# One core: windowed attention, downsampled attention and an MLP; 128x128 transposes for four pairs, group sums by selection matrices, a longer ring for the MLP's input, other places for transposes and weights

## Chip, cores and metric

The kernel runs on one core of one Trainium2 chip. The metric is the device time of one execution, in microseconds. TensorE (PE in the profile) multiplies, VectorE (DVE), ScalarE (ACT) and GpSimd (POOL) do elementwise work, and SyncE (SP) issues most DMAs. A DMA can be issued from SP's, ACT's or POOL's instruction queue; all of them share 16 DMA engines.

## What is computed

q, k and v are (8, 8, 576, 64) in float32: batch, heads, positions, width of a head. Two attentions are added and an MLP follows:

```python
q_d = q.reshape(B, H, Sd, factor, D).mean(axis=3)       # factor 4, Sd = 144; k_d, v_d alike
out_up = np.repeat(sm_attn(q_d, k_d, v_d), factor, axis=2)
mask = np.abs(pos[:, None] - pos[None, :]) < factor     # a band of 7
scores = np.where(mask, scale * np.matmul(q, k.transpose(0, 1, 3, 2)), -1000000000.0)
attn_out = out_up + np.matmul(softmax(scores), v)
x = attn_out.transpose(0, 2, 1, 3).reshape(B * S, H * D)   # 4608 x 512
h = x @ w_in                                             # 512 x 2048
out = (h * sigmoid(h)) @ w_out                           # 2048 x 512
```

## The kernel before

**Pairs.** The 64 heads are taken as 32 pairs p of two heads; four pairs make one batch element, that is 576 rows of the MLP's input. For each pair q and k are loaded in float32 (qk), cast to bf16 (qkb), transposed on TensorE (job T, 36 transposes of 64x64, L813) and evicted by ACT and DVE as qT and kT. From these come sums over groups of four positions, qd and kd: for pairs 0 to 11 on TensorE (job G, eight matmuls with an identity, 144 columns each, which read qT and kT), for the others on DVE (L848). Job S computes the scores of the band and of the downsampled part into two PSUM banks; ACT takes the exponentials (Pt and Pd, L896). For pairs 0 to 7 the mask is added in PSUM by four matmuls with 288 columns before the scores; for the others DVE multiplies Pt by a 0/1 mask (L902). Job Z makes the sums of the softmax, whose reciprocals DVE spreads (zt, zr, Rb, L967 to L977). Job PV multiplies by v. DVE scales the product into xo (L993), and POOL adds the two attentions into xT (L1021), the MLP's input, transposed.

**v.** v is loaded twice: in windows of 64 positions (vs, cast to vb on POOL) for the band, and, for pairs 8 and up, in groups of four positions (vq), which POOL sums in two steps (vt, L787, and vd, L792). For pairs 0 to 7 these sums come from vb on TensorE (job VP, nine matmuls).

**MLP.** The 4608 rows are nine tiles of 512. For each tile, 16 units g1 (four 128x512 matmuls each, float32) give the columns of h; ACT takes a tanh (L1047), DVE makes gT of it (L1051). Another 16 units g2 (four 128x512 matmuls in bf16) give the output, which ACT copies out of PSUM (L1079). xT is a ring of XR = 1536 rows, three tiles. A g1 of tile j needs the xT of all pairs of the batch elements that the tile touches: tile 1 needs pairs up to 7, tile 2 up to 11, tile 3 up to 15.

**Order.** Nothing is scheduled at run time. A planner in the kernel (class Plan) holds jobs with costs, due times, pools of buffers and PSUM banks, plays them through, and the instructions of each engine are emitted in the order that it finds; each engine and each queue then runs strictly in that order. DMAs have planned durations (the argument `work`: 0.85 us for q or k of a pair, 0.39 for a quarter of v's windows, 3.2 for a quarter of w_in or w_out), and code has a planned time to be fetched (FETCH), for every 256 instructions of TensorE. Where the plan has TensorE idle early in the run, it puts in matmuls on a constant tile dz, which are thrown away.

Pairs 0 to 7 run as separate jobs. From pair 8 on, one job per pair, the visit V(n), puts S of pair n, T of pair n+1, PV of pair n-2 and Z of pair n-1 together. A visit may run once 8(n - 10) MLP units have been issued.

**Loads.** q and k of a pair are 128 partitions of 576 elements each; k is shifted by half a pair, so that the first pair needs an extra piece, kx. Pairs 1 to 3 are loaded with a cast by the DMA, from POOL's queue (SW). v's windows go to 64 partitions per DMA. The weights go out from POOL's queue; each of the eight parts (w0 to w3 of w_in, w4 to w7 of w_out) waits for a named load of v (W_GATE). The loads of pair 8 wait on SP's queue until w2 has landed.

Of the kernel before, what the change touches and what calls it, by code (L numbers as in the profile page):

```python
# [7 lines left out]
ALU = mybir.AluOpType  # L8
# [10 lines left out]
XR = 1536  # L19
COLD = (8.0, 1.65)  # L20
WARM_END, WARM_GAP, WARM_PART, WARM_COLD = 115.0, 0.4, 0.6, 7.0
FETCH = (4.5, 110.0, 3.7)
N_QK, N_VS, N_VQ, N_QKB, N_VB, N_VD, N_T, N_P, N_ZR, N_RB, N_XO = 3, 4, 2, 5, 5, 5, 3, 4, 2, 4, 2
GS_PE = 12
# [3 lines left out]
CAST2 = 4  # L28
SW = (1, 2, 3)
MB = 8  # L30
LAG = 2
THR0 = 10
# [28 lines left out]
def G1_BANKS(j):  # L61
    return ((6,), (7,), (5,)) if j == 0 else ((6,), (7,), (0,), (1,)) if j == 8 else ((6,), (7,))


def T_BANKS(p):
    return ((4,), (5,), (6,), (7,)) if p < 4 else ((4,), (5,))
# [18 lines left out]
W_GATE = {0: ("lv211",), 1: ("lv511",), 2: ("lv611",), 3: ("lv711",), 4: ("lvq8",), 5: ("lvq9",), 6: ("lvq10",), 7: ("lvq11",)}  # L85
# [6 lines left out]
def load_order():  # L92
    o = ["kx", ("qk", 0), ("qk", 1), ("qk", 2), ("qk", 3), ("v", 0), ("v", 1), ("v", 2), ("v", 3)]
    for p in range(4, NPAIR):
        o += [("qk", p), ("v", p)] + ([("vq", p)] if p >= VP_PE else [])
    return o, {**{p: ["lv311!"] for p in range(4, 8)}, 8: ["w2"]}
# [8 lines left out]
def LD_ENG(x, p):  # L105
    return ("SP", "ACT") if p in (1,) else "SP"
# [388 lines left out]
def bass_hourglass_attn__then__act_silu_kernel(  # L495
# [9 lines left out]
    with kctx:  # L505
# [26 lines left out]
        vq = sb("vq", [128, 4, 256], F32, N_VQ)  # L532
        vt = sb("vt", [128, 4, 128], F32)
        qkb = sb("qkb", [128, 2, 576], BF16, N_QKB)
# [4 lines left out]
        qd = sb("qd", [128, SD], BF16, N_T)  # L539
        kd = sb("kd", [128, 192], BF16, N_T)  # L540
# [6 lines left out]
        for name, n, first in (("qk", N_QK, 0), ("vs", N_VS, 0), ("vq", N_VQ, VP_PE), ("vt", 1, VP_PE),  # L547
                               ("qkb", N_QKB, -1), ("vb", N_VB, 0), ("vd", N_VD, 0), ("T", N_T, 0), ("P", N_P, 0),
                               ("zr", N_ZR, 0), ("Rb", N_RB, 0), ("xo", N_XO, 0), ("th", 2, 0), ("osb", 2, 0)):
            L.pool(name, n, first, SW if name == "qk" else ())  # L550

# [5 lines left out]
        mbias = sb("mbias", [128, 2, 288], BF16)  # L557
        nidn = sb("nidn", [128, 64], BF16)
# [25 lines left out]
        ci, ri = region(1792, 64)  # L584
        kx, rkx = region(2048, 576)
        cpv = cp.rearrange("p (a b) -> p a b", a=2)
        cmv = cm.rearrange("p (a b) -> p a b", a=5)
        CH, CK, CB, CM0, CW, CO, CO2, CE0, CE1, CP_, CM1 = range(11)
# [19 lines left out]
        def fill(name, parts, due, eng=("DVE", "POOL")):  # L608
# [3 lines left out]
            J(name, eng, {"DVE": 0.1 * len(parts), "POOL": (0.14 if name != "rwz" else 0.5) * len(parts)}, emit, due=due)  # L612

        def constants():
            rW = [R(f"hot{i}") for i in range(3)]
            iota("cp", col(CP_), [[1, 1]], 0, 1, rc(CP_), 0.2, -100)
            iota("ci", ci, [[-1, 64]], 0, 1, ri, 0.25, -99)
# [6 lines left out]
            ts("idn", idn[:, :], ci, col(CB), ALU.add, 0.0, ALU.is_equal, rc(CB) + ri, [R("idn")], 0.26,  # L624
               ["ci", "cb"], -98)
# [3 lines left out]
            ts("ce0", col(CE0), col(CP_), 3.0, ALU.is_ge, 1.0, ALU.mult, rc(CP_), rc(CE0), 0.15, ["cp"], 40)  # L629
            ts("ce1", col(CE1), col(CP_), 123.0, ALU.is_lt, 1.0, ALU.mult, rc(CP_), rc(CE1), 0.15, ["cp"], 40)  # L630
# [6 lines left out]
            fill("idwz", [(idw[:, :], 0.0, [], [R("idw")])], -82, "POOL")  # L637
            for j in range(2):
                const(f"idw{j}", "DVE", 0.14, lambda e, j=j: e.tensor_copy(
                    idw[half(j), 64 * j:64 * j + 64], idn[half(j), :]), r=[R("idn"), R("idw")], w=[R("idw")],  # L640
                    pre=["idn", "idwz"] + ["idw0"] * j, due=-81)
            for i, (a, b, c, rr) in enumerate(((0, 58, col(CE0), rc(CE0)), (58, 232, 1.0, []),
                                               (232, 288, col(CE1), rc(CE1)))):
                ts(f"mask{i}", mask[:, a:b], cm[:, a:b], 3.0, ALU.is_le, c, ALU.mult, rr + rm, [R(f"mask{i}")], 0.24,
                   ["cma"] + (["ce0", "ce1"] if rr else []), 41)
            ts("cm0", col(CM0), col(CK), 3.0, ALU.is_lt, 100.0, ALU.mult, rc(CK), rc(CM0), 0.15, ["ck"], -94)
            ts("cm1", col(CM1), col(CK), 59.0, ALU.is_ge, 100.0, ALU.mult, rc(CK), rc(CM1), 0.15, ["ck"], -94)
            ts("nidn", nidn[:, :], idn[:, :], -81920.0, ALU.mult, 0.0, ALU.add, [R("idn")], [R("nidn")], 0.17, ["idn"], -85)
            for i, (y, a, b, c) in enumerate(((0, 0, 58, CM0), (0, 58, 288, None), (1, 0, 232, None), (1, 232, 288, CM1))):
                if c is None:  # L650
                    ts(f"mb{i}", mbias[:, y, a:b], cm[:, a:b], 3.0, ALU.is_gt, 1.0, ALU.mult, rm, [R(f"mb{i}")], 0.42,
                       ["cma"], -84)
                else:
                    ts(f"mb{i}", mbias[:, y, a:b], cm[:, a:b], col(c), ALU.add, 3.0, ALU.is_gt, rc(c) + rm, [R(f"mb{i}")],
                       0.3, ["cma", "cm0", "cm1"], -84)
# [10 lines left out]
            for i in range(N_VQ):  # L666
                fill(f"vqz{i}", [(vq[i][:, t, :], 0.0, [], [R(f"vqc{i}{t}")]) for t in (1, 3)], 100)
# [5 lines left out]
        def rows(t, p, n, off):  # L673
            return bass.AP(tensor=t.tensor, offset=t.offset + (128 * p + off) * 576, ap=[[576, n], [1, 576]])
# [7 lines left out]
        def loads(p, order):  # L682
            if p == 0:
# [118 lines left out]
        def t_home(p, x, r):  # L802
            return bank(("qk"[x], p))[0], 32 * r
# [481 lines left out]
```

## Time and profile before

| | us |
|---|---|
| three runs | 367.11, 366.29, 366.30 |
| median | 366.3 |
| profiled execution | 365.78 |
| its span in the profile | 364.0 |

Busy time by stage, from the stretches of the trace. The first stage ends with the first transposes, the second with the scores of pair 4, the third with the first visit (pair 8), the fifth holds two visits, and the sixth ends with the last transposes.

| stretch, us | PE busy | DVE busy | ACT busy | POOL busy | clock | GB/s |
|---|---|---|---|---|---|---|
| 0 to 8.96 | 5.52 | 5.67 | 3.71 | 6.32 | 1.00 | 176 |
| 8.96 to 30.28 | 17.53 | 14.40 | 9.86 | 9.97 | 0.84 | 238 |
| 30.28 to 61.09 | 29.20 | 21.26 | 18.89 | 18.53 | 1.00 | 251 |
| 61.09 to 141.08 | 77.02 | 65.73 | 48.50 | 63.18 | 1.00 | 236 |
| 141.08 to 162.04 | 13.16 | 6.63 | 6.12 | 13.51 | 0.76 | 235 |
| 162.04 to 240.29 | 77.54 | 59.15 | 44.99 | 40.62 | 1.00 | 118 |
| 240.29 to 364.00 | 119.69 | 47.35 | 47.17 | 4.82 | 1.00 | 43 |

The clock is the share of full speed that TensorE was granted. GB/s is what all DMAs moved. In the timeline views a row has the start, the duration, the engine, the line, the operation with what it writes and reads, and in brackets how long the engine stood idle before it and which event ended that. Rows of SPq are the issuing of DMAs on SP's queue. Rows follow program order within an engine, and neighbours of one form are merged.

### The profile page before, as it was taken

The numbers are of one execution on the slowest core, as the hardware profiler recorded it, in microseconds if no ns is written. First come the engines' busy times: TensorE is split into PE (matmuls) and PEld (weight loads), VectorE is DVE, ScalarE is ACT, GpSimd is POOL, SyncE is SP. The second block draws the span as 40 slices with busy tenths as digits, with TensorE's granted clock in tenths as the row PEclk, the third lists the DMA queues.
The fourth block names the chain that finished last, engine by engine and source line by source line (L and its number), as shares of the span: only waits on it lengthen the run. The fifth ranks groups of instructions, "written<-read, shape, count | busy, mean of one in ns | idle before, by whom it ended". The sixth has DMA issues, their size and how long they took to land.

```text
span 364.0 us, 10850 instructions
## 1 busy us (share of the span) xinstructions
PE 339.7 (93%) x4674; PEld 217.9 (60%) x4709; DVE 220.2 (60%) x398; ACT 179.2 (49%) x328; POOL 156.9 (43%) x183
## 2 busy tenths in 40 slices
PE   6969899999989999199999999999999999999996
PEld 2747677676556666066666666666665666655542
DVE  6667577668887795257868786776544233433300
ACT  4625566666465566045565546554344343444311
POOL 6349258768986863956658535100310000000000
PEclk9898999999999999779999999999999999999999
DMA  8999999999978786988873100000001001100112
GB/s 177 175 296 252 211 289 247 250 262 272 264 207 231 216 237 175 273 226 234 223 239 96 68 31 33 31 31 29 31 31 58 30 31 41 46 29 31 57 60 86
DMA packets 70522, 52.78 MB, mean 145 GB/s; under 512 B 45898, under 2 KB 56394, under 8 KB 70474
## 3 DMA queue, kind: packets, MB, share of 16 engines
q1 hardware_dynamic: 64378, 44.66, 44.6%
q0 software_dynamic: 5088, 7.18, 9.1%
q8 instruction: 37, 0.61, 0.7%
q10 hardware_dynamic: 1008, 0.25, 0.3%
q14 instruction: 11, 0.09, 0.1%
HBM read 45.61 MB, written 9.44 MB: 151 GB/s over the span
## 4 chain that ended last, share of the span: by engine, by line
PE 87%; DVE 4%; DMA 3%; issue 3%; ACT 2%; POOL 0%; SPq 0%; DVEq 0%; ACTq 0%; POOLq 0%
PE PS L571 84%; DMA qk<-in_k_dram 3%; PE PS L813 3%; DVE xo L993 1%; DVE gT L1051 1%; ACT th L1047 1%; DVE Rb L977 1%; POOL xT L1021 0%; ACT Pt L896 0%; ACT qT L565 0%; ACT osb L1079 0%; SPq L678 0%; DVE zt L967 0%; ACT qkb L565 0%; DVE zr L971 0%
## 5 line engine op out<-in xcount | busy, mean ns | idle before, releaser
L571 PE MATMUL PS<-xT,w_in_sb 128*128 128x512 f32 x576 | 164.5, 422 | 8.7 <-DVE gT L1051 8.5
L1051 DVE SCALAR_TENSOR_TENSOR gT<-th,PS 128x512 bf16<-128x512 f32 x144 | 97.2, 681 | 86.0 <-ACT th L1047 81.3
L1047 ACT ACTIVATE th<-PS 128x512 f32<-128x512 f32 x144 | 86.3, 600 | 109.5 <-PE PS L571 109.3
L571 PE MATMUL PS<-w_out_bf,gT 128*128 128x512 bf16 x547 | 131.1, 381 | 3.3 <-ACT qT L565 1.0
L571 PEld LDWEIGHTS PS<-xT,w_in_sb 128*128 128x128 f32 x576 | 106.8, 191 | 38.1 <-DVE gT L1051 11.0
L571 PEld LDWEIGHTS PS<-w_out_bf,gT 128*128 128x128 bf16 x576 | 51.2, 98 | 70.3 <-issue 14.0
L1021 POOL TENSOR_TENSOR xT<-xo 128x576 fp32r<-128x576 f32 (+3 forms) x48 | 42.8, 908 | 60.7 <-DVE xo L993 31.0
L1079 ACT ACTIVATE osb<-PS 128x512 f32<-128x512 f32 x36 | 21.5, 597 | 46.7 <-PE PS L571 46.7
L774 POOL CAST qkb<-qk 128x1152 bf16<-128x1152 f32 x28 | 33.0, 1178 | 11.8 <-DMA qk<-in_k_dram 11.8
L993 DVE TENSOR_TENSOR xo<-PS,Rb 128x720 f32<-128x720 f32 x32 | 28.7, 896 | 14.9 <-POOL xT L1021 9.1
L565 POOL CAST vb<-vs 128x640 bf16<-128x640 f32 x32 | 23.2, 727 | 28.8 <-PE PS L571 17.4
L787 POOL TENSOR_TENSOR vt<-vq 128x512 f32<-128x512 f32 x24 | 31.5, 1313 | 4.8 <-DMA vq<-in_v_dram 4.6
L977 DVE STREAM_TRANSPOSE Rb<-zr 128x768 f32<-128x768 f32 x32 | 30.9, 966 | 0.2
L896 ACT ACTIVATE Pt<-PS 128x576 bf16<-128x576 f32 x32 | 20.7, 647 | 5.5 <-PE PS L571 5.5
L565 ACT ACTIVATE qT<-PS 128x576 bf16<-128x576 bf16 x30 | 19.9, 667 | 5.2 <-PE PS L813 5.2
L813 PE MATMUL PS<-idn,qkb 64*64 64x64 bf16 x1152 | 16.3, 196 | 3.6 <-ACT qkb L565 2.0
L792 POOL TENSOR_TENSOR vd<-vt 128x256 bf16<-128x256 f32 x24 | 18.2, 759 | 0.0
L902 DVE TENSOR_TENSOR Pt<-Pt,mask 128x576 bf16<-128x576 bf16 x24 | 16.6, 691 | 2.6 <-ACT Pt L896 2.6
L565 ACT ACTIVATE kT<-PS 128x576 bf16<-128x576 bf16 x27 | 17.9, 663 | 0.0
L896 ACT ACTIVATE Pd<-PS 128x432 bf16<-128x432 f32 x32 | 17.2, 536 | 0.0
L813 PEld LDWEIGHTS PS<-idn,qkb 64*64 64x64 bf16 x1152 | 13.1, 110 | 4.9 <-ACT qkb L565 2.1
L571 PE MATMUL PS<-Pd,vd 64*64 64x72 bf16 (+1 forms) x256 | 14.3, 201 | 0.5 <-issue 0.5
(64 smaller groups left out, 230.9 us busy)
## 6 DMA issues: line engine op xcount, KB each, us to landing
vs<-in_v_dram SPq DMA_DIRECT2D x123, 80.0 KB, 4.5
out_dram<-osb SPq DMA_DIRECT2D x36, 256.0 KB
qk<-in_q_dram SPq DMA_DIRECT2D x29, 288.0 KB, 4.2
qk<-in_k_dram SPq DMA_DIRECT2D x28, 288.0 KB, 5.0
vq<-in_v_dram SPq DMA_DIRECT2D x24, 256.0 KB
w_in_sb<-in_moe_w_in_dram POOLq DMA_DIRECT2D x4, 1024.0 KB, 8.6
w_out_bf<-in_moe_w_out_dram POOLq DMA_DIRECT2D x4, 512.0 KB, 9.7
vq<-in_v_dram SPq DMA_DIRECT2D x48, 32.0 KB
```

The costliest lines, as they stand in the source:

```text
L565: return e.activation(out_, in_, AF.Copy) if eng == "ACT" else e.tensor_copy(out_, in_)
L571: P.op("PE", lambda t: t.matmul(out_, lhsT, rhs, start=start, stop=stop, skip_group_check=True), r, w)
L774: P.op("POOL", lambda e, a=i(), b=j(): e.tensor_copy(qkb[b][:, :, :], qk[a][:, :, :]), [R(f"qk{i()}0"), R(f"qk{i()}1")], [R(f"qkb{j()}0"), ...
L787: P.op("POOL", lambda g: g.tensor_tensor(vt[:, :, :], vq[n][:, :, 0:128], vq[n][:, :, 128:256], ALU.add), [R(f"vqm{n}"), R(f"vqe{n}0"), R( ...
L813: P.op("PE", lambda e, o=o, w=w, j=j: e.transpose(o, w, idn[half(j), :]), [R("idn"), R(f"qkb{n}{x}")], [rB[t]])
L896: P.op("ACT", lambda e: e.activation(d[:, :, :], PS[:, b[0]:b[1] + 1, a:e_], AF.Exp, scale=sc), [rB[b[0]], rB[b[1]]], [R(f"P{m}" if local ...
L977: P.op("DVE", lambda e: e.transpose(Rb[n][:, :].rearrange("p (c q) -> p c q", q=32), zr[z][:, :].unsqueeze(2).to_broadcast([128, 24, 32])) ...
L993: P.op("DVE", lambda e: e.tensor_tensor(xo[x][:, :, :], PS[:, bb[0]:bb[1] + 1, 0:360], Rb[u][:, :].rearrange("p (x c) -> p x c", x=2)[:, : ...
L1021: P.op("POOL", lambda g, dst=dst, in0=in0, in1=in1: g.tensor_tensor(dst, in0, in1, ALU.add), [R(f"xo{x}")], xblk(kc, t + a, t + e_))
L1047: P.op("ACT", lambda e: e.activation(th[x][:, :], PS[:, b, :], AF.Tanh, scale=0.5), [rB[b]], [R(f"th{x}")])
L1051: P.op("DVE", lambda e: e.scalar_tensor_tensor(gT[j % 2][:, f, :], th[x][:, :], 1.0, PS[:, b, :], ALU.add, ALU.mult), [rB[b], R(f"th{x}")] ...
L1079: P.op("ACT", lambda e, s=S("osb", n), b=bank(key)[0]: e.activation(osb[s][:, :], PS[:, b, :], AF.Copy, scale=0.5), [rB[bank(key)[0]]], [R ...
```

## The change

- Layout of loads: q of a pair goes to partitions 0 to 63 and k to partitions 64 to 127, the two heads side by side in the free dimension (128 runs of 2304 bytes, as before). The shift of k, the extra piece kx and the casting loads of pairs 1 to 3 are gone; those pairs are cast on POOL. qkb is laid out as [128, 9, 2, 64], so that for each of nine positions both heads are 128 contiguous columns.
- T of pairs 0 to 3 is nine transposes of 128x128, into two banks (E, F or G, H); the others keep 36 of 64x64.
- G reads qkb instead of qT and kT: nine matmuls with 288 columns, by nine selection matrices `sel`, made on DVE at the start (in the memory that vq uses later). It is used for pairs 0 to 7 (GS_PE 12 to 8); pairs 8 to 11 take DVE's sums. One copy of 288 columns takes the place of two of 144.
- The mask bias is two matmuls of 128 rows and 288 columns instead of four of 64 rows.
- From pair 4 on, T is a job of its own, in the score banks 0 and 1, and may run once 8(p - 10) - 12 MLP units have been issued. g1 may use banks 4 to 7 instead of 6 and 7.
- XR is 2048: four tiles.
- W_GATE: w1 to w4 each wait for an earlier load of v than before, and w5 to w7 follow w4 at once. Pair 8's loads wait for w3.
- vt is gone: POOL's first sum over vq is written in place. Pools: four vd for five, four T for three, two Rb for four.
- The planner's DMA durations of loads and weights are multiplied by DSLOW = 1.2, its code fetch times are longer (FETCH), and two rules of its choice among TensorE's jobs are gone.

```diff
-XR = 1536
+XR = 2048
-FETCH = (4.5, 110.0, 3.7)
-N_QK, N_VS, N_VQ, N_QKB, N_VB, N_VD, N_T, N_P, N_ZR, N_RB, N_XO = 3, 4, 2, 5, 5, 5, 3, 4, 2, 4, 2
-GS_PE = 12
+FETCH = (5.2, 110.0, 4.5)
+DSLOW = 1.2
+N_QK, N_VS, N_VQ, N_QKB, N_VB, N_VD, N_T, N_P, N_ZR, N_RB, N_XO = 3, 4, 2, 5, 5, 4, 4, 4, 2, 2, 2
+GS_PE = 8
+TW = 3
-CAST2 = 4
-SW = (1, 2, 3)
+CAST2 = 1
+TAHEAD = 12
 def G1_BANKS(j):
-    return ((6,), (7,), (5,)) if j == 0 else ((6,), (7,), (0,), (1,)) if j == 8 else ((6,), (7,))
+    return ((6,), (7,), (0,), (1,)) if j == 8 else ((6,), (7,), (5,), (4,))
 def T_BANKS(p):
-    return ((4,), (5,), (6,), (7,)) if p < 4 else ((4,), (5,))
+    return ((0,), (1,)) if p > TW else (EF, GH) if p < 4 else (EF,)
-W_GATE = {0: ("lv211",), 1: ("lv511",), 2: ("lv611",), 3: ("lv711",), 4: ("lvq8",), 5: ("lvq9",), 6: ("lvq10",), 7: ("lvq11",)}
+W_GATE = {0: ("lv211",), 1: ("lv411",), 2: ("lv511",), 3: ("lv611",), 4: ("lv711",), 5: ("w3!",), 6: ("w4!",), 7: ("w5!",)}
-    return o, {**{p: ["lv311!"] for p in range(4, 8)}, 8: ["w2"]}
+    return o, {**{p: ["lv311!"] for p in range(4, 8)}, 8: ["w3"]}
 def LD_ENG(x, p):
-    return ("SP", "ACT") if p in (1,) else "SP"
+    return ("SP", "ACT") if (x, p) == ("v", 1) else "ACT" if (x, p) == ("k", 0) else "SP"
...
+            for i in range(9):
+                ts(f"sel{i}", sel[:, i, :], ci, ch_[:, i:i + 1], ALU.is_equal, 1.0, ALU.mult, ri + rh, [R(f"sel{i}")], 0.45,
+                   ["ci", "cgf"], -80)
...
-        def rows(t, p, n, off):
-            return bass.AP(tensor=t.tensor, offset=t.offset + (128 * p + off) * 576, ap=[[576, n], [1, 576]])
+        def rows(t, p):
+            return bass.AP(tensor=t.tensor, offset=t.offset + 128 * p * 576, ap=[[576, 64], [64 * 576, 2], [1, 576]])
...
         def pe_T(p):
+            n = S("qkb", p)
+            if wide(p):
+                b = bank(("t", p))
+                for r in range(9):
+                    o = PS[:, b[r // 8], 64 * (r % 8):64 * (r % 8) + 64].bitcast(BF16)
+                    P.op("PE", lambda e, o=o, r=r: e.transpose(o, heads(n, r), idw[:, :]),
+                         [R("idw"), R(f"qkb{n}0"), R(f"qkb{n}1")], [rB[b[r // 8]]])
+                return
...
         def pe_G(p):
-            s, b = S("T", p), bank(("g", p))[0]
-            for x, t in enumerate((qT[s][:, :], kT[s][:, 3:579])):
-                for r in range(4):
-                    mm(PS[:, b, 144 * x:144 * x + 144], idw[:, :], t.rearrange("p (g r) -> p r g", r=4)[:, r, :],
-                       [R("idw"), R(f"{'qk'[x]}T{s}")], [rB[b]], r == 0, r == 3)
+            n, b = S("qkb", p), bank(("g", p))[0]
+            for r in range(9):
+                mm(PS[:, b, 0:288], heads(n, r), sel[:, r, :], [R(f"sel{r}"), R(f"qkb{n}0"), R(f"qkb{n}1")], [rB[b]], r == 0, r == 8)
...
                 for h in range(2):
-                    for y in range(2):
-                        mm(PS[half(y), bb[h], 0:288], nidn[half(h), :], mbias[half(h), y, :],
-                           [R("nidn")] + [R(f"mb{i}") for i in range(4)], [rB[bb[h]]], True, False)
+                    mm(PS[:, bb[h], 0:288], idw[:, :], mbias[:, :], [R("idw"), R("mbias")], [rB[bb[h]]], True, False)
...
+        def one_T(p):
+            J(f"T{p}", "PE", 0.7 if wide(p) else 0.42 if p <= SPLIT else 0.55, lambda jb: pe_T(p), mm=9 if wide(p) else 36, kind="A" if p <= SPLIT else "T", due=D(p, 8.5),
+              thr=8 * (p - THR0) - TAHEAD, take=[("T", p)] if p > SPLIT else [], **tk(p))
+            after_T(p)
```

In the program that this gives, the first visit's scores stand after 17 MLP units (16 before), those of pairs 9, 13, 17 and 20 after 35, 59, 87 and 104 units (20, 40, 61 and 76 before); the filler matmuls are 20 for 29, the last four of them just before the first visit.

## The prediction

> **What bounds the kernel now.** I read the slices first, to see where TensorE is not at work, then the two timelines around the holes, then stretches by stage.
>
> ```profile
> PE 339.7 (93%) x4674; PEld 217.9 (60%) x4709; DVE 220.2 (60%) x398; ACT 179.2 (49%) x328; POOL 156.9 (43%) x183
> ...
> PE   6969899999989999199999999999999999999996
> ...
> PEclk9898999999999999779999999999999999999999
> DMA  8999999999978786988873100000001001100112
> GB/s 177 175 296 252 211 289 247 250 262 272 264 207 231 216 237 175 273 226 234 223 239 96 68 31 33 31 31 29 31 31 58 30 31 41 46 29 31 57 60 86
> ```
>
> TensorE is the bound almost everywhere; slice 17 (146 to 155 us) is empty, and its clock is low there and after. The early slices are thinner too, and the DMA engines are full up to about 100 us.
>
> ```profile
> 140.28 0.43 SPq L678 DMA_DIRECT2D qk<-in_k_dram  x1
> ...
> 145.15 1.14 POOL L774 CAST qkb<-qk 128x1152 bf16<-128x1152 f32 x1 [5.50 <-DMA qk<-in_k_dram]
> 145.41 0.43 SPq L678 DMA_DIRECT2D qk<-in_k_dram  x1
> ...
> 149.60 1.14 POOL L774 CAST qkb<-qk 128x1152 bf16<-128x1152 f32 x1 [0.75 <-DMA qk<-in_k_dram]
> 150.71 2.37 POOL L1021 TENSOR_TENSOR xT<-xo 128x576 fp32r<-128x576 f32 x2
> ...
> 152.01 0.91 DVE L993 TENSOR_TENSOR xo<-PS,Rb 128x720 f32<-128x720 f32 x1 [9.10 <-POOL xT L1021]
> ...
> 154.96 3.78 PE L571 MATMUL PS<-xT,w_in_sb 128*128 128x512 f32 x8 [7.73 <-DVE gT L1051]
> ```
>
> This is the big hole, read backwards. TensorE waits 7.73 us for gT; DVE, in order, has stood 9.10 us before an xo product, for want of an xo buffer; POOL, in order too, stood before two casts whose q and k had not landed, with the xT sums that free xo queued behind them. So a late load of a pair needed later stops work that was ready. Then eight matmuls take 3.78 us (2.11 at 142.5): the clock row is 0.50 to 159.5 us, which is another 2.4 us. Together 10.1 us.
>
> ```profile
> 8.22 0.68 ACT L565 ACTIVATE qkb<-qk 128x576 bf16<-128x576 f32 x1 [2.81 <-DMA qk<-in_k_dram]
> ...
> 19.76 0.41 PE L571 MATMUL PS<-Pd,vd 64*64 64x72 bf16 x6 [0.47 <-issue]
> ...
> 25.90 0.18 PE L571 MATMUL PS<-Pt,vb 64*64 64x56 bf16 x1 [2.62 <-issue]
> ...
> 43.44 0.31 PE L813 MATMUL PS<-idn,qkb 64*64 64x64 bf16 x14 [1.29 <-issue]
> ```
>
> Counting a weight load and a matmul as one instruction each in program order, the "issue" waits (with 0.31 at 35.83) stand at instructions of about 702, 958, 1470 and 1726: a grid of 256. The queue of instruction loads has 37 loads, 0.61 MB, for TensorE's 9,383 instructions. So these are waits for code, 4.7 us, with a half clock (0.50) from 26.3 to 30.3 behind the longest, about 2 us more. The time from one such point to the next is 4.9 to 7.6 us where it decides.
>
> **Prices on TensorE at full clock** (start of one block to the next in the timeline): an MLP unit of four 128x512 matmuls 0.91 us (49 matmuls in 11.15); 36 small transposes T 0.31; group sums G 0.94 (46.47 to 47.41); scores with mask bias 0.50; sums Z 0.37; VP 0.62; PV 0.40; a late visit 1.44. Check: up to the first visit at 61.09 the work is 8 pairs x 3.14 = 25.1, T and G of pair 8 1.25, 16 units 14.6, start 8.96: 49.9, so 11.2 us are waits and slow clock. From there to the end (361.5) 272 units are 247.5 and the visits 35.0, three G 2.8, thirteen filler matmuls 2.9: 288.2 of 300.4, so 12.2 us are lost, 10.1 of them in the big hole.
>
> **The change, part by part.**
>
> *Wide transposes, pairs 0 to 3.* 9 instead of 36, so 54 instructions fewer each, 216 in all. The trace has no 128x128 transpose; nearest is VP, nine matmuls with 128 columns at 0.62. By the 36 small ones as floor 0.31, by G's 0.117 each as ceiling 1.05; I take 0.62, so +1.2 us on TensorE for four.
>
> *Group sums by selection matrices.* Nine matmuls over 288 columns in place of eight over 144, for 8 pairs, not 12. A 512-column one takes 0.2275, so 288 take 0.128, and nine 1.1 us (floor 0.94 as now, ceiling 1.4): +1.3 over 8 pairs, and G of pairs 8 to 11 is gone: -3.8. G now reads qkb, not the evicted qT and kT, so it no longer waits for 1.3 us of evictions before each early score block. Pairs 8 to 11 pay two DVE sums of 0.71 each, less a 0.31 copy: 4.4 us on DVE, which is 82% busy from 61 to 141 (65.73 of 79.99) with TensorE then idle only 3 us; I count nothing, 2 us if the cover is gone. Bias: two 288-column matmuls for four concurrent quarter ones, 0.25 for 0.15, +0.8.
>
> *Loads.* The kx load (0.74) and the six casting loads on POOL's queue (2.09 to 5.46) go; q0 and k0 go out first, on SP and ACT. Now k0 goes out third and lands 6.22 later. First issues here landed after 3.1 (half the size) to 6.2; I take 4.5, so casts at 5.3 and T0 at 6.6, for DVE makes six of nine selection matrices before its cast (0.33 to 0.66 each by the vsel and mbias rows). The first G, at half clock, is twice its price, so of 2.4 us gained at T0 I keep 1.0 at the first scores (-2.5 to +1). Casts of pairs 1 to 3 on POOL, 3 x 1.15, fall into its idle 6.95 to 14.03; the memsets of vq, 1.54, move behind the last G into POOL's idle 38.3 to 45.2, with casts behind them.
>
> *w_out ahead of pair 8.* POOL issues w_in's last part and the four of w_out in a row (0.78 each, in the same idle time). SP's queue, with everything of pair 8 and on behind it, waits for w_in3 and not w_in2. It stood 9.8 us until 43.44, and then the DMA engines were empty (share 0.08 at 42 to 44). Pairs 0 to 7 and w_in are 11.7 MB; at 255 to 277 GB/s (the rate of 18 to 42 us) they are in by 46 to 49 us. Pair 8 took 17.7 us from issue to its visit, with 8 us of that unforced; so the visit is at 57 to 62.
>
> *First stage, summed.* Start 6.6, four pairs at 3.7 and four at 3.4, T 0.3, 17 units 15.5: 50.8. Of 11.2 us lost I leave 8: fewer code points (the fourth pair ends near instruction 800, not 1100) but fillers and the wait for pair 8. First visit at 58.8 with 17 units done, 57.9 by the old 16: **-3.2**.
>
> *Later stages.* G of pairs 9 to 11 **-2.8**; thirteen fillers fall to four, which stand before the visit and were counted: half of 2.9 is **-1.4**, since part of it was waiting anyway. The planner's DMA times are now 20% longer: before, a late pair of 1.25 MB was planned at 4.1 us (305 GB/s), while the stretches from 60 to 100 us moved 248 to 270; now 253. So casts stand in POOL's order nearer to when they can run, and the ring of 2048 lets xT sums go on further ahead: the hole **-10.1**.
>
> *New waits.* Transposes now use the score banks: scores, two exponentials 1.19, T 0.31, two evictions 1.34, a DVE sum 0.7 and four handovers make some 4.6 us between visits, and the tightest new visits (4 units apart) leave 4.9; a tanh of 0.6 in between costs its length. Attention also runs 15 to 20 units later: MLP tile 2 needs pair 11, and all 64 earlier units are used up just as it comes. Pair 13's scores (at 105 us) stand before that, and want by some 95 us pairs 0 to 7 7.3 MB, w_in 4.2, w_out 2.1, five and a half later pairs 6.9, seven outputs 1.8, code 0.4: 22.7 MB, where the old order had moved 24.5 by 100 (the GB/s row): slack of about 2 us at worst, 6 at best. Pair 9's vq load must wait on SP's queue for pair 8's to land, once, some 4.5 us, ahead of all later loads. Rb has two buffers for four. I take **+4** (0 to 10).
>
> Sum: 364.0 - 3.2 - 2.8 - 1.4 - 10.1 + 4 = 350.5 span. The profiled execution took 365.8, 1.8 more than its span, and the median of the runs shown is 0.5 above that: **352.8**, say 352.5.
>
> [...]
>
> **Rivals.**
>
> *A hole of the old kind comes back* (a load late by some us with sums queued behind it, around w_out's loads or tile 2). For it: the DMA share is 0.9 to 1.2 to 100 us, and slack is 2 to 6 us. Against: loads are ordered by a rate that the trace shows. It costs 5 to 10 more: 357 to 363.
>
> *Half-partition loads are slower.* q goes to partitions 0 to 63 only and k to 64 to 127, where each took 128. If such a load ran at half rate, the 8.3 MB of q and k that pair 13 needs would take 31 us longer at 265 GB/s, of which slack covers 6: 25 on top of 352.5, 377. It decides once it costs more than 14, that is 22.7 MB at under some 210 GB/s. Against: v's loads go to 64 partitions already, and the DMA engines move 250 and more with them.
> [...]
>
> *All of it works*: new waits 0, first stage -6: 345 to 346.
>
> *The early part gains nothing* because loads, not code, pace it: 355 to 356, still in the forecast's band.
>
> **Chances.** Forecast band 348 to 357 0.52; better 0.14; a hole again 0.19; half-partition loads or a starved tile 2 that costs more than the 14 gained 0.15, of which 0.03 ends within 0.3% (1.1 us, about what a measurement can tell). So faster 0.85, same 0.03, slower 0.12. Range 345 to 363.
>
> **What would show it.** Right: no idle of over 3 us on TensorE after 100 us, POOL's casts waiting less than 2 us on loads; G at about 1.1 us and wide T at 0.6; first visit near 59; "issue" waits under 3 us. Wrong: q and k landing later than the 4.2 to 5.0 us of now, TensorE idle around 60 to 110 us before pair 8 or MLP tile 2.

## The result, and the profile after

| | us |
|---|---|
| changed kernel, four runs | 375.29, 377.4, 378.57, 379.5; median 377.99 |
| kernel before, four runs | median 366.34 |
| ratio | 1.0305, 95% interval 1.0242 to 1.0367 |
| profiled execution, its span | 375.29, 373.1 |

Slower by 3.1%, where 352.5 was forecast. The page after (TensorE's row, the slices of 9.3 us, one queue's share, and the median us from issue to landing of q and k):

```profile
PE 343.0 (92%) x4508; PEld 214.6 (58%) x4552; DVE 228.1 (61%) x400; ACT 177.7 (48%) x313; POOL 156.9 (42%) x192
...
PE   6687899999998698979996999999999999999996
...
PEclk9999899999999899989998999999999999999999
DMA  8999989948987999988899452120000100010112
GB/s 180 198 245 236 267 184 219 220 118 213 233 220 205 236 213 222 198 231 217 189 236 273 120 134 89 46 68 28 32 28 30 56 28 30 37 47 30 38 74 84
...
q1 hardware_dynamic: 64746, 46.06, 51.2%
...
qk<-in_q_dram SPq DMA_DIRECT2D x32, 288.0 KB, 4.9
...
qk<-in_k_dram SPq DMA_DIRECT2D x31, 288.0 KB, 5.5
```

The one empty slice is gone, and in its place TensorE is thinned out in many (slices 13, 14, 16, 18 and 22, within 112 to 205 us). The loads carry less: from 60 to 80 and 80 to 100 us all DMAs moved 196 and 191 GB/s, before 248 and 270. Queue q1 carries what SP issues, the loads of q, k and v and the stores. Before, the page had

```profile
q1 hardware_dynamic: 64378, 44.66, 44.6%
```

Now the queue took 51.2% of 16 engines for 46.06 MB; times the span that is 0.512 x 373.1 / 46.06 = 4.15 us of 16 engines for a MB, before 0.446 x 364.0 / 44.66 = 3.64. So each MB costs 14% more of the engines' time. That is not all: the engines were also less busy, at a share of 1.03 and 0.80 in these two stretches where it was 1.19 and 1.07 before.

The first pairs in the timeline (start, duration, engine, line, operation, and the idle time before with its end):

```profile
6.83 0.67 PE L807 MATMUL PS<-idw,qkb 128*128 128x128 bf16 x9 [0.63 <-DVE qkb L568]
7.34 1.27 PE L574 MATMUL PS<-vqa,qkb 128*128 128x288 bf16 x9
10.14 0.68 PE L807 MATMUL PS<-idw,qkb 128*128 128x128 bf16 x9 [1.53 <-POOL qkb L763]
10.66 1.27 PE L574 MATMUL PS<-vqa,qkb 128*128 128x288 bf16 x9
11.76 0.41 PE L574 MATMUL PS<-mbias,idw 128*128 128x288 bf16 x2
```

From block to block the wide T takes 0.51 (6.83 to 7.34), G 1.10, the bias 0.34. But T1 waits 1.53 us for its cast on POOL, T2 1.00 and T3 1.06. The first visit comes at 68.94 with 17 units done (61.09 with 16 before). Now SP's queue, with the ACT and POOL rows that belong to it:

```profile
72.86 0.60 SPq L681 DMA_DIRECT2D qk<-in_q_dram  x1
73.50 0.61 SPq L681 DMA_DIRECT2D qk<-in_k_dram  x1
74.15 1.93 SPq L707 DMA_DIRECT2D vs<-in_v_dram  x3
...
81.35 0.60 ACT L1080 ACTIVATE osb<-PS 128x512 f32<-128x512 f32 x1 [2.87 <-PE PS L574]
81.97 0.38 SPq L681 DMA_DIRECT2D out_dram<-osb  x1
82.39 0.60 SPq L707 DMA_DIRECT2D vs<-in_v_dram  x1
...
84.67 0.60 SPq L681 DMA_DIRECT2D qk<-in_q_dram  x1
85.05 0.72 POOL L568 CAST vb<-vs 128x640 bf16<-128x640 f32 x1 [5.52 <-DMA vs<-in_v_dram]
```

The first output store stands on SP's queue from 76.08, and what it stores is ready at 81.95. Behind it stands the last quarter of a v load that is already out by three quarters; POOL waits 5.52 us for it, with the casts of later pairs behind. Pair 11's q goes out at 84.67, 11.8 us after pair 10's. (Pair 10's had itself gone out 12.8 us after pair 9's, with no store between: four loads of v took SP 6.24 us there, and it waited 2.5 us before a vq load.) The loss reaches TensorE at 124 us:

```profile
119.53 0.72 POOL L568 CAST vb<-vs 128x640 bf16<-128x640 f32 x1 [1.47 <-DMA vs<-in_v_dram]
...
122.09 1.26 POOL L778 TENSOR_TENSOR vqa<-vqa 128x512 f32<-128x512 f32 x1 [1.83 <-DMA vqa<-in_v_dram]
123.31 1.20 POOL L1022 TENSOR_TENSOR xT<-xo 128x576 fp32r<-128x576 f32 x1
...
124.56 0.50 PE L574 MATMUL PS<-xT,w_in_sb 128*128 128x512 f32 x1 [3.28 <-POOL xT L1022]
```

This is the form of the old hole, smaller: an xT sum stands on POOL behind work that waits for v (1.47 and 1.83 us), TensorE has used up all its units and waits 3.28 us, and the clock sags behind it (0.91 from 120 to 140). TensorE waits again at 145.46 (1.74 us, for a cast of POOL), 165.35 (1.85) and 199.56 (3.29).

### The profile page after: what moved, and what is told of

Read it like the earlier page. It is cut to its first block, busy times and chain, and to the rows that moved or that the text cites. A ratio compares the mean times of both kernels' runs of the same rounds, so it can differ in the third digit from the quotient of the medians.

```text
span 373.1 us, 10580 instructions
## 1 busy us (share of the span) xinstructions
PE 343.0 (92%) x4508; PEld 214.6 (58%) x4552; DVE 228.1 (61%) x400; ACT 177.7 (48%) x313; POOL 156.9 (42%) x192
## 3 DMA queue, kind: packets, MB, share of 16 engines
q1 hardware_dynamic: 64746, 46.06, 51.2%
## 4 chain that ended last, share of the span: by engine, by line
PE 54%; DMA 17%; SPq 12%; POOL 8%; issue 5%; DVE 1%; ACT 0%; POOLq 0%; DVEq 0%; ACTq 0%
PE PS L574 53%; DMA vqa<-in_v_dram 7%; DMA qk<-in_k_dram 6%; SPq L707 5%; DMA vs<-in_v_dram 4%; SPq L681 3%; SPq L721 3%; POOL vqa L778 2%; POOL xT L1022 2%; SPq L717 2%; POOL qkb L763 2%; POOL vd L783 1%; PE PS L815 1%; POOL vb L568 1%; ACT osb L1080 0%
## 5 line engine op out<-in xcount | busy, mean ns | idle before, releaser
L574 PE MATMUL PS<-xT,w_in_sb 128*128 128x512 f32 x576 | 170.1, 428 | 9.6 <-POOL xT L1022 9.6
L574 PEld LDWEIGHTS PS<-xT,w_in_sb 128*128 128x128 f32 x576 | 107.4, 192 | 39.3 <-POOL xT L1022 11.8
L574 PEld LDWEIGHTS PS<-w_out_bf,gT 128*128 128x128 bf16 x576 | 49.2, 98 | 66.2 <-issue 17.3
L1022 POOL TENSOR_TENSOR xT<-xo 128x576 fp32r<-128x576 f32 (+5 forms) x48 | 43.0, 909 | 32.2 <-DVE xo L994 32.1
L763 POOL CAST qkb<-qk 128x1152 bf16<-128x1152 f32 x31 | 35.7, 1150 | 34.8 <-DMA qk<-in_k_dram 34.8
L778 POOL TENSOR_TENSOR vqa<-vqa 128x512 f32<-128x512 f32 x24 | 30.8, 1282 | 23.2 <-DMA vqa<-in_v_dram 23.2
L994 DVE TENSOR_TENSOR xo<-PS,Rb 128x720 f32<-128x720 f32 x32 | 28.6, 895 | 11.9 <-PE PS L574 11.8
L568 POOL CAST vb<-vs 128x640 bf16<-128x640 f32 x32 | 22.9, 722 | 12.4 <-DMA vs<-in_v_dram 12.3
L852 DVE TENSOR_REDUCE qkd<-qT 128x144 bf16<-128x576 bf16 x24 | 17.5, 727 | 9.0 <-ACT qT L568 9.0
L783 POOL TENSOR_TENSOR vd<-vqa 128x256 bf16<-128x256 f32 x24 | 17.9, 746 | 9.9 <-PE PS L574 9.2
L815 PEld LDWEIGHTS PS<-idn,qkb 64*64 64x64 bf16 x1008 | 10.7, 111 | 14.5 <-issue 4.7
L852 DVE TENSOR_REDUCE qkd<-kT 128x144 bf16<-128x576 bf16 x24 | 17.5, 731 | 0.0
L815 PE MATMUL PS<-idn,qkb 64*64 64x64 bf16 x1008 | 13.9, 198 | 3.5 <-POOL qkb L763 1.7
```

The costliest lines, as they stand in the source:

```text
L568: return e.activation(out_, in_, AF.Copy) if eng == "ACT" else e.tensor_copy(out_, in_)
L574: P.op("PE", lambda t: t.matmul(out_, lhsT, rhs, start=start, stop=stop, skip_group_check=True), r, w)
L763: P.op("POOL", lambda e, a=i(), b=j(): e.tensor_copy(qkb[b][:, :, :, :].rearrange("p r h d -> p h r d"), qk[a][:, :, :].rearrange("p h (r ...
L778: P.op("POOL", lambda g: g.tensor_tensor(a, a, b, ALU.add), vr(n), [R(f"vqs{n}")])
L815: P.op("PE", lambda e, o=o, w=w, x=x: e.transpose(o, w, idn[half(x), :]), [R("idn0"), R("idn1"), R(f"qkb{n}0"), R(f"qkb{n}1")], [rB[t]])
L852: P.op("DVE", lambda e: e.tensor_reduce(dst, src.rearrange("p (g r) -> p g r", r=4), AX.X, ALU.add), [R(f"{'qk'[x]}T{s}")], [R(f"{'qk'[x]} ...
```

## The experiments

Ratios are to the kernel before, measured beside each run on the same chip, with their 95% interval; its median was 366 to 369 us there. "Full rows", the halves in the kernel before and the first even/odd run mix rows: scores are then taken between wrong rows of q and k, with every instruction otherwise as it was.

**Full rows in the changed kernel, halves in the kernel before.** Two runs, each with the order of all engines unchanged. (In the kernel before, the casts of single tiles then also wait for both loads of a pair.)

```diff
-  [[576, 64], [64 * 576, 2], [1, 576]]  into  qk[...][half(x), :, :]
+  [[576, 128], [1, 576]]                into  qk[...][:, x, :]
```

> The changed kernel, same order on every engine, but q and k of a pair again go to all 128 partitions each, one row of 2304 bytes per partition, instead of q to 0..63 and k to 64..127. It puts rows of q and k in other places than the transposes want, so the scores are those of mixed rows; the work and its order are unchanged. Layout theory (a load to half of the partitions is slower: in the changed kernel SP issues one in 0.61 us instead of 0.43 and the DMA share per MB of SP's queue is 11% higher): issue back to 0.43, first visit at 62 to 65 us instead of 68.9, time 364 to 370. Order theory (the gate on w3, the vq buffers and the output stores in SP's queue make the loads late): first visit within 1 us of 68.9, time 376 to 379.

> The kernel before, same order, with q and k of pairs 0 and 4 to 31 loaded to half of the partitions each, two rows of 2304 bytes per partition (the rows then stand in other places than the transposes want; the work is unchanged). Layout theory: slower than before by 5 to 12 us, the hole near 146 us longer, landing times of q and k up by 0.5 us or more. Order theory: 366 to 368.

Full rows: 363.51 us, 0.9873 [0.978, 0.9966]. Halves put into the kernel before: 379.27, 1.0294 [1.0215, 1.0374]. The two go opposite ways by 4.3 and 2.9%. With full rows the page has

```profile
q1 hardware_dynamic: 64746, 46.06, 45.9%
...
qk<-in_q_dram SPq DMA_DIRECT2D x32, 288.0 KB, 4.3
...
qk<-in_k_dram SPq DMA_DIRECT2D x31, 288.0 KB, 5.1
```

which is 0.459 x 361.9 / 46.06 = 3.61 us for a MB, against 4.15; the halves in the kernel before took 0.495 x 377.0 / 44.81 = 4.17:

```profile
q1 hardware_dynamic: 64442, 44.81, 49.5%
```

So the layout is a cause. It leaves 361.7 (0.9873 x 366.3) where 352.5 was forecast. The rate is no sign of the layout alone: with full rows 60 to 80 us moved only 128 GB/s, while SP stood 12.4 us before a store.

**The planner's slower transfers alone**, in the kernel before.

```diff
-  0.85 * n / 128   (and the other durations of loads)
+  0.85 * DSLOW * n / 128,  DSLOW = 1.2
```

> The kernel before with one thing of the change: the planner's DMA durations times 1.2, so only the order of instructions on the engines and the fillers differ. If the hole at 146 us comes from an order made with too fast loads, as the prediction held: no idle of over 3 us on TensorE after 100 us and 354 to 360 us. If the order is not what makes the hole, or the fillers and the later visits that the longer durations bring cost as much: 364 to 370.

360.91 us, 0.98 [0.972, 0.9879], and again below; after 100 us no wait of TensorE is over 1.7 us. So planning with slower transfers cures the big hole.

**The weight gates.** Before's W_GATE, and pair 8 behind w2: once in the changed kernel, once with full rows as well.

```diff
-W_GATE = {..., 1: ("lv411",), ..., 5: ("w3!",), 6: ("w4!",), 7: ("w5!",)};  8: ["w3"]
+W_GATE = {..., 1: ("lv511",), ..., 5: ("lvq9",), 6: ("lvq10",), 7: ("lvq11",)};  8: ["w2"]
```

> The changed kernel with the gates of before: w1 to w3 one load of v later, w_out gated by pairs 8 to 11's vq loads, pair 8 waiting for w2. The order follows the new plan. Order theory: pair 8's loads go out near 44 us instead of 54.4, first visit near 62, time 368 to 373. Layout theory: loads stay late, and w_out now lands late as well, so TensorE waits after 32 units: 376 to 385.

> The changed kernel with the q and k loads over all 128 partitions (rows mixed as in the run with full rows), and besides with the weight gates of the kernel before: w_in pieces after the v loads of pairs 2, 5, 6, 7, w_out after the sums' loads of pairs 8 to 11, pair 8 waiting for the third piece of w_in. Everything else of the change is kept and the order is planned anew. Theory A (what is left of the miss after the layout, 363.5 against a forecast of 352.5, is mostly the first stage, held up by weights that were moved ahead of pair 8): pair 8's loads go out at 43 to 45 us instead of 47.7, the first visit is near 61 instead of 66, and the time is 356 to 359 us. Theory B (the first stage is held by the POOL casts and the code waits, and weights only take other bytes' place): first visit at 64 to 67 us, time 361 to 366 us.

In the changed kernel 371.93, 1.0111 [1.0015, 1.0208], first visit 63.66 for 68.94. With full rows 361.32, 0.9839 [0.9753, 0.9925], against 0.9873 without: no difference that the intervals allow to be told, though the first visit moved from 65.96 to 62.34. So the gates cost 2% with halves and nothing that shows with full rows.

**Even and odd partitions.** Same order, same rows to as many partitions, only other ones:

```diff
-  qk[S("qk", p)][half(x), :, :]
+  qk[S("qk", p)][x:128:2, :, :]
```

> The changed kernel, instruction for instruction in the same order; only the partitions differ to which the q and k loads write: q of a pair goes to the 64 even partitions and k to the 64 odd ones, instead of q to the lower half and k to the upper half. Number of loads, rows per load, bytes per row and partitions per load (64) stay. The rows of q and k are then interleaved in the tiles that are transposed and grouped, so scores are taken between mixed rows. [...]

371.7 us, 1.0167 [1.0079, 1.0256]: neither the time of full rows (363.51) nor that of halves (377.99). The page says what came back and what did not:

```profile
q1 hardware_dynamic: 64746, 46.06, 44.8%
...
qk<-in_q_dram SPq DMA_DIRECT2D x32, 288.0 KB, 4.2
...
qk<-in_k_dram SPq DMA_DIRECT2D x31, 288.0 KB, 4.8
```

The transfer is at 0.448 x 368.0 / 46.06 = 3.58 us for a MB, as with full rows, and landing too. The issue on SP is 0.62, as with halves (0.43 with full rows). What differs between halves and this is which 64 partitions; so the transfer's price lies in their lying side by side. But only 1.4% of time came back (1.0305 to 1.0167, whose intervals just overlap) of the 4.3% that full rows gain with the same order and the same transfer. The rest goes with two rows for each of 64 partitions. The longer issue fits it: from pair 11's q to pair 16's SP takes 34.45 us here and 32.38 with full rows, and ten issues that are 0.19 longer make 1.9. That it is the reason is not shown.

A MB costs more in adjacent halves (4.15 us) and not on every second partition (3.58; full rows 3.61); why, no run shows. All of q1 loses 15% a MB; q and k, 63 loads of 288 KB, are 18.6 of its 46.06 MB, and if they bear all of it, a MB of theirs costs some 37% more (an estimate from 4.15, 3.61 and these sizes).

**Stores from ACT's queue.** In this run and the one with full rows SP stood over 12 us before the first store, so the next runs move the 36 stores to ACT, which makes what they store. The order of TensorE, DVE and POOL is kept in both.

```diff
-  P.op(j.ran, lambda s: s.dma_start(out_(), in_()), ...)
+  P.op("ACT" if name[:3] == "out" else j.ran, lambda s: s.dma_start(out_(), in_()), ...)
```

> The changed kernel with one difference: its 36 output stores are issued from ACT's queue, behind the copy that feeds them, instead of from SP's. The order of TensorE, DVE, POOL and of all that is left on SP is the same; ACT's has the stores added (0.33 us each on SP). Nothing of the computation differs. Theory A (in the changed order a store stands on SP's queue before its data are ready, with loads behind it: SP stood 5.9 us before the first store at 76 us, and later pairs' casts and xT sums waited for those loads): loads of pair 11 and on go out some 6 us earlier, TensorE's waits on POOL's xT fall from 9.6 to under 4 us, and the time is 366 to 372 us. Theory B (the transfers themselves, at 191 to 196 GB/s from 60 to 100 us, are the limit, and an earlier issue only queues them earlier): 375 to 380 us.

> The changed kernel with the q and k loads over all 128 partitions (rows mixed as in the run with full rows, 363.5 us) and the 36 output stores issued from ACT's queue instead of SP's; all else in the same order. There SP stood 12.4 us before the first store, and the stretch from 60 to 80 us moved 128 GB/s. Theory A (that stop is what makes the 3.8 us wait for a cast at 134 us and the low clock behind it): GB/s of 60 to 80 us back over 220, no wait on POOL's qkb or xT over 1.5 us after 100 us, 354 to 359 us. Theory B (the rest of the miss is the first stage alone, first visit at 66 instead of 58.8, and the loads are early enough): 361 to 366 us.

The changed kernel with this alone: 365.43 us, 0.9933 [0.9891, 0.9975], against 1.0305. With full rows as well: 356.19, 0.9682 [0.9613, 0.9752]. SP's queue in the first of the two (its profiled execution took 369.3, the longest of its ten):

```profile
69.66 0.61 SPq L681 DMA_DIRECT2D qk<-in_q_dram  x1
70.31 0.61 SPq L681 DMA_DIRECT2D qk<-in_k_dram  x1
...
76.10 0.60 SPq L681 DMA_DIRECT2D qk<-in_q_dram  x1
76.75 0.60 SPq L681 DMA_DIRECT2D qk<-in_k_dram  x1
...
82.01 0.60 SPq L681 DMA_DIRECT2D qk<-in_q_dram  x1
```

In these rows a pair goes out every 6 us, with no gap of 11.8, and all DMAs move 229 and 230 GB/s from 60 to 80 and 80 to 100 us although the layout is still that of halves. So the low rates of the changed kernel there came of the store too. TensorE's waits at 124, 145 and 165 us are gone, and the one near 200 is left (5.1 us at 193.6). The first visit is later than in the changed kernel (72.27 for 68.94) in this faster run, so what the stores cost lies behind it. With full rows 60 to 80 us move 252 GB/s, and no wait of TensorE after 100 us is over 0.9. Theory A of both runs holds (365.43 lies just under its range); its sign of small xT waits does not in the first run's profile (6.5 us).

**The same in the kernel before**, with the planner's slower transfers, and these alone once more.

> The kernel before, planned with the DMA durations times 1.2, and its 36 output stores issued from ACT's queue instead of SP's; all else in the same order. It computes all that the reference does. Theory A (stores and waits on SP hold loads there too: 3.9 us before stores, 6.1 before vq loads from 60 to 200 us): 1 to 4 us faster than the same kernel with the stores on SP, in the same call. Theory B (loads run far enough ahead, and ACT, which makes the exponentials and tanh, loses 12 us of issuing): 0 to 3 us slower.

> The kernel before, planned with the DMA durations times 1.2 alone, once more and in more rounds, as the one that the run with the stores on ACT is compared with, and to see how far the 2.0% by which it was faster holds on another chip and day. Theory A (the gain is that of a better order): a ratio of 0.975 to 0.988 to the kernel before. Theory B (single runs of these kernels move by a per cent or more with when holes happen to fall): 0.99 to 1.00.

359.87, 0.9795 [0.9743, 0.9847], against 361.11, 0.9815 [0.9756, 0.9875]: nothing gained there. Its first store goes out at 96.2 us (81.97 in the changed kernel), and SP stood 3.9 us before stores from 60 to 200 us in the first profile of that kernel. So it is in the changed order, in which outputs come sooner and loads later, that the stores on SP's queue hurt. The gain of 2% repeats.

**Even and odd set right, stores from ACT.** The readers of the tile follow the layout, so all of the reference is computed; the gates of the kernel before are the second run's one difference. The small transposes' evictions now read both banks, and the planner makes another order of it than the changed kernel's: pair 1's transposes come before pair 0's group sums, and TensorE waits 0.78 us for the first casts and not 3.6.

```diff
-  "p (r x g) -> p x g r"                      (eviction, wide T)
+  "p (r g x) -> p x g r"
-  t = bank(("qk"[x], p))[0]                   (small T: one bank for q, one for k)
+  t = x                                       (one bank for each half of the partitions)
-  group = (9 * partition + r) >> 2            (sel)
+  group = (9 * (partition >> 1) + 576 * (partition & 1) + r) >> 2
```

> The changed kernel with q on the 64 even and k on the 64 odd partitions of a pair's tile, this time with all that reads the tile set to it (the selection matrices, the 64x64 transposes by halves of the partitions, the evictions that part q from k), so that it computes all that the reference does; and the 36 output stores on ACT's queue. [...] An eviction of the small transposes now reads both banks. With the stores on ACT the changed kernel took 0.993 of the kernel before, and with full-width loads as well 0.968. Theory A (what the layout costs is the transfer): 0.965 to 0.975, 354 to 358 us, q1 near 45% of the engines' span. Theory B (it is SP's issue of 0.60 instead of 0.43 us, 63 times): 0.985 to 0.995, 361 to 366 us, with q1 near 45% all the same. In between, both count.

> As the run with the right even and odd partitions and the stores on ACT, and besides the weight gates of the kernel before (w_out after pair 8, pair 8 waiting for the third piece of w_in). Theory A (the gates that put w_out ahead of pair 8 hold the first visit back by some 5 us, as between 68.9 and 63.7 us in the changed kernel and that with the gates before): first visit 4 to 6 us earlier and 3 to 6 us faster than the run without the gates, 350 to 354 us. Theory B (once the loads run at the full rate, the first visit is no limit, since with full-width loads the gates made 363.5 into 361.3 us, within the intervals): within 2 us of it, either way.

356.67 us, 0.9612 [0.955, 0.9675]; with the gates of before 361.19, 0.976 [0.9697, 0.9823]. The queue without stores, with halves, with full rows and in the first of these two runs:

```profile
q1 hardware_dynamic: 59562, 36.62, 45.3%
...
q1 hardware_dynamic: 59562, 36.62, 39.0%
...
q1 hardware_dynamic: 59562, 36.62, 39.5%
```

Times the spans of 367.0, 355.1 and 354.8 us that is 4.54, 3.78 and 3.83 us for a MB. So the first run has the issue time of halves (0.61 to 0.62) and the transfer of full rows, and it takes the time of full rows: as theory A, the transfer, has it. With the stores off SP's queue the longer issue is then no cost that can be seen; since the order differs too, that it costs nothing is not shown. And w_out ahead of pair 8 costs nothing here; the gates of before are slower. The first run's slices:

```profile
PE   7977999999999999999989999999999999999996
...
PEclk9987999999999999999999999999999999999999
...
GB/s 228 193 258 270 241 220 263 248 232 235 226 227 265 204 228 204 265 199 239 189 267 190 152 101 68 34 31 59 22 40 31 30 30 61 30 30 31 59 60 89
```

TensorE is full from slice 5 (35 us) to the last but for slice 21, and the clock sags only early.

**The ring and the sums in place.** Each was put alone into the kernel before with the planner's slower transfers, and undone in the run with even and odd partitions.

```diff
 f3:  XR 1536 -> 2048, Rb 4 -> 2            f4:  first sum into vq itself, vt gone
 i1:  XR 2048 -> 1536                       i2:  as i1, and vt back
```

> The kernel before, planned with the DMA durations times 1.2 (360.9 us alone), and besides the MLP ring of 2048 columns instead of 1536, with two Rb buffers instead of four to make room, as the change has it. Nothing else. Theory A (the ring lets the MLP's units run further ahead, which is what the planner's slower transfers need): 354 to 359 us. Theory B (with the hole gone the ring is no limit; the visits are set by loads and casts): 359 to 363 us. If two Rb buffers hold the visits up, 364 us or more with PE waits on DVE's Rb or xo.

> The kernel before, planned with the DMA durations times 1.2 (360.9 us alone), and besides the first sum of v's groups written over its own input, as the change has it, so that a vq buffer comes free only after the second sum. PE's order differs in one place by three pairs of MLP units. Theory A (the held vq buffers stop SP's queue, whose q and k loads stand behind the vq load: in the changed kernel SP waited 16 to 20 us for the second sum): SP's waits on POOL's vd reach 10 us or more and the time rises by 3 to 8 us, to 364 to 369 us. Theory B (those waits are slack that SP has anyway, since it runs ahead): 359.5 to 362.5 us.

> As the run with the right even and odd partitions and the stores on ACT (0.961 of the kernel before), with the MLP's ring back at 1536 columns and nothing else; it computes all that the reference does. The order is planned anew, since the ring frees later. Theory A (the longer ring is worth nothing or harms, as it did in the order of the kernel before, where it made 0.980 into 1.009): 0.950 to 0.963. Theory B (in the changed order, where transposes stand outside the visits, POOL's xT sums do need the fourth tile): 0.97 to 0.99, with TensorE's waits on POOL's xT or casts over 3 us between 100 and 200 us.

> As the run with the short ring, and in the memory that this frees the buffer vt is back, so that a vq buffer comes free after the first of POOL's two sums instead of the second. Theory A (the sums in place cost the changed order what they cost the kernel before with the planner's slower transfers, 0.980 against 1.002): 1 to 3 per cent faster than the run with the short ring, SP's waits on the second sum gone. Theory B (with the stores on ACT SP's queue has the slack for these waits, and the changed order is no faster for it): within 1 per cent of it.

Put in: the ring 369.13, 1.0086 [1.0044, 1.0129], and the sums in place 367.04, 1.002 [0.9968, 1.0071], both against 0.9815. Undone: the short ring 360.89, 0.9802 [0.975, 0.9855], against 0.9612, and with vt as well 353.37, 0.9633 [0.959, 0.9676]. So the sums in place cost some 2% in both orders. In the new order SP's waits go with it: 20.3 us for the second sum in the run with the short ring, and 10.3 us for the two sums with vt. In the old order SP waited 11.7 us with the sums in place and 8.2 and 11.0 in the two profiles without, so there the way into the time is open. These waits with them, and without in one of the two:

```profile
SPq L723 <- POOL vd L793: 11.7, 6, 5.9
...
SPq L723 <- POOL vt L788: 6.7, 4, 5.0
...
SPq L723 <- POOL vd L793: 1.5, 2, 0.9
```

The ring goes both ways: it costs 3% in the old order (with a wait of 5.0 us of TensorE for ACT's osb) and gains 2% in the new one. Why it costs in the old one is open; the order changed with it, and it came with two Rb buffers for four. The long ring with vt was not run.

## Why the prediction was wrong

**The step that failed first** is the one under "Loads": q0's and k0's landing was worked out there, and the layout of the other 62 loads was left at nothing, as a rival at 0.15 or less. In the same order it cost 4.3%, some 16 us. The reason given against the rival, that v's loads go to 64 partitions already and the DMA engines move 250 with them, doesn't carry: with q and k in halves too, a MB takes 14% more. The rival's own point was "under some 210 GB/s" to 100 us, and 196 and 191 were measured, but with the stores moved the same layout reaches 229 and 230. Its time was 377, from half the rate for q and k; the layout cost less than that, and the stores made up the rest. That the price fits 377.99 is luck.

**The other half** is the stores: 3.7% in the same order, some 14 us. The rival of the hole named its form (a load late, with sums queued behind it), but no step and no rival named a store. "New waits +4" counts POOL, the score banks and a vq load on SP's queue, but not that w_out ahead of pair 8 lets the first outputs come early in the plan, and so makes SP stand before a store from 76 us on, ahead of loads of pairs that run later than planned. (Full rows: the first store goes out at 79.0 us with the new gates, at 97.3 with those of before.)

| ratio to before | stores on SP | stores on ACT |
|---|---|---|
| q and k in halves | 1.0305 | 0.9933 |
| over all 128 partitions | 0.9873 | 0.9682 |
| even and odd | 1.0167 (rows mixed) | 0.9612 (another order) |

Undoing the layout gains 4.3%, the stores 3.7%, both 6.2% in the same order: 0.9682 x 366.3 = 354.6 us, where 352.5 was forecast. The right kernel with even and odd takes 0.9612 x 366.3 = 352.1, in an order of its own. That the terms are right does not follow from either: some cost more and some less, as below.

**By its terms**, in the run with even and odd set right: the span was to be 350.5, first visit at 58.8, and 291.7 from there. It was 354.8, 65.1 and 289.7 (355.1, 66.5 and 288.6 with full rows and the stores on ACT).

- *First stage -3.2*: wrong; in no run with the change did the first visit come before 62.3 us. In the changed kernel T0 came at 6.83 and the first scores at 12.1, 1.2 us earlier, as priced (6.6, 1.0), though the clock under the first G (7.34 to 8.61) was 1.00 and not half. Then POOL's casts took it back (T1 to T3 waited 3.6 us), code waits went on (1.27 at 32.14 and 1.48 at 41.59; 5.1 us to the end, under 3 was the sign), and pair 8's loads went out at 54.38 (49.34 with even and odd; 46 to 49 was priced). From there the visit took 15 to 16 us and not the 11 to 13 that "8 us unforced" was to leave.
- *Wide T 0.62, G 1.1, bias +0.1*: 0.51, 1.10, and a bias of 0.34 where 0.25 was taken. Right but for 0.7 us (8 pairs x 0.09).
- *G of pairs 9 to 11 and fillers, -4.2; the hole, -10.1*: for the hole right in kind. The planner's slower transfers alone took it out and gained 2.0% (7 us). No run tests the first two alone.
- *New waits +4*: in the changed kernel 304.2 us lie behind the first visit, 12.5 more than the sum; with even and odd 2.0 less. So the term was mis-sized: it lacks the store, and it has the sums in place (2%) as one wait of 4.5 us where SP waited 19.6 us in ten. What it named besides, no run parts from the rest.
- *The ring lets sums go on further ahead*: the run with the short ring bears it out, 2%.
- *Half-partition loads are slower*: for adjacent halves this rival was right against the forecast (4.15 us for a MB against 3.61 over all 128 partitions). Two interleaved halves took 3.58.
- *What would show it*: of the signs of "wrong" one was seen, q and k landing after 4.9 and 5.5 us (4.2 and 5.0). TensorE idle at 60 to 110 us was not; its two waits of 3.3 us came at 124 and 199 us. That POOL's casts wait little on loads was no good sign of "right": they waited 34.8 us in 20 times, but 25.9 in the run with even and odd set right too (11.8 before).

## What to carry to other kernels

When the partitions of a load change, count its bytes again at another rate: here 64 partitions spread over all 128 took 3.58 us of 16 engines for a MB, as all 128 did (3.61), and 64 side by side 4.15. On a queue that runs in order, an instruction that waits for results (a store) should not stand ahead of loads that are needed soon: SP stood 5.9 us before the first store, and 12.4 with full rows. Issue it from the engine that makes the result, which gained 3.7% in the changed kernel. Where the order left the loads slack, that gained nothing (0.9795 against 0.9815). And where a planner orders a queue, a change that makes one thing early and another late shows up there first, so read the queue's order of both kernels before pricing the engines.

## What was not expected of the hardware

A load of q or k took SP 0.61 us to issue (the median in the changed kernel) with two rows to each of 64 partitions, and 0.43 (the median with full rows) with one to each of 128. With the stores on ACT this cost nothing that can be seen (0.9612 and 0.9682); with the stores on SP's queue 2.9% lies between two runs with the same transfer, and the issue may be its reason. The transfer took 4.15 us of 16 engines for a MB in the changed kernel, 3.61 with full rows and 3.58 with even and odd partitions. With the stores on SP, even and odd partitions gain 1.4% by it; with the stores on ACT, full rows gain 2.5%, issue and transfer together. v's loads go to 64 adjacent partitions in all these kernels; whether they too would gain was not tried.
